# Another order and other engines for the same operations in an attention and feed-forward kernel

## The chip, the cores and the metric

The kernel runs on one core of one Trainium2 chip. The metric is the device time of one execution in microseconds (us), start-up and end included; the profile shows one such execution of its own. The engines are PE (matmuls; PEld are its weight loads), DVE, ACT, POOL and SP. Each works through its own queue in order, and semaphores hold an instruction back until what it needs is there.

## The reference

Eight batches of eight heads, 576 rows, head size 64. Attention is taken over 32 landmarks (means of 18 rows), with the inverse of the 32x32 middle matrix by six steps of an iteration; the result goes through a layer norm and a feed-forward block of width 2048, and is added to itself.

```python
def _attn_ref(q, k, v):
    ...
    q_lm = q.reshape(B, H, m, S // m, D).mean(axis=3)
    k_lm = k.reshape(B, H, m, S // m, D).mean(axis=3)
    ...
    A = sm(q, k_lm)
    Bm = sm(q_lm, k_lm)
    C = sm(q_lm, k)
    ...
    for _ in range(6):
        Z = 2 * Z - Z @ Bm @ Z
    return (A @ Z @ C @ v).astype(np.float32)

def _moe_ref(x, g_ln, w_ch1, w_ch2):
    ...
    xn = (x - mu) / np.sqrt(var + 1e-06) * g_ln
    ch = np.maximum(xn @ w_ch1, 0.0) @ w_ch2
    return (x + ch).astype(np.float32)
```

## The kernel before

The program first defines 1571 named operations, each with the engines that may do it, the buffers that it uses and a function that emits its instructions. A list, ORDER, then names them one by one: a number (the operation's place among the definitions) and a letter for its engine (P, D, A, G and S for PE, DVE, ACT, POOL and SP). The loop at the end of the kernel emits the operations in that list's order, and every engine keeps its instructions in it:

```python
    names = list(OPS)
    order = [(names[int(x[:-1])], x[-1]) for x in ORDER.split()] if ORDER else [(n, OPS[n][0][0]) for n in names]
    for n, e in order:
        emit(n, e)
```

The list sets the buffers too. Each kind of buffer has a number of slots; the first use of a buffer takes the slot that has been free longest, and its last use gives it back, both in the order of the list. PSUM has two slots of two banks (kind p2) and four of one bank (kind bank), so a PE operation that takes a slot waits for the DVE or ACT operation that empties it. Six slots (stg) serve first q, k and v of batch 0, then the tiles of the first weight, then sums of the second.

Batch 0 is loaded by SP and cast to fp16 (cast, tile nat). PE turns it (turns, tiles pst to xT) and sums it by landmark (sums, tile pss), DVE makes qbd from the sums, PE multiplies the landmarks into the first bank of the iteration (psb, tile it). Six steps of the inverse go back and forth between PE (step) and DVE (next). They end in zt and zc (tiles pszt and pszc), of which DVE makes zcbd. rows (psy) gives the attention's rows, x_ copies them out, measure takes the variance. The other batches are worked in sets of one or two in the same manner, beside the feed-forward of batches already there.

For the first matrix of the feed-forward, w1 is loaded in eight tiles (w1s), each scaled in two halves (scale, tile w) and its column means are formed on PE (less_mean, psf) and taken out by ACT (less). psm multiplies the small attention matrix into w1, m16 evicts it (on DVE with less for batches 0 and 1), psh multiplies it by the attention weights ea, and relu evicts that into hT. For batches 0 and 1 the second matrix is multiplied block by block (pso, then done on DVE). From batch 2 on, four blocks at a time are multiplied as a 2x2 problem with seven products instead of eight (seven; tiles ps7a, ps7c, ps7e), for which sums of parts of hT are formed first (hmix, on DVE or POOL, line 207) and sums of the second weight once (mix). norm divides ea by its sums (after ln and inv on ACT). The last block of all is written in two parts, 384 and 128 columns (pso_74a and pso_74b), and stored from SP, ACT or POOL (line 223).

Helpers record most operations, so many have one line: 193 matmuls, 200 copies and casts, 203 activations, 207 tensor_tensor, 210 scalar_tensor_tensor, 223 DMAs. Some matmuls work on tiles of the array of 32x32, 64x32 or 64x64, the others on the whole of it. A few matmuls on zeros (warm, tile idle) keep PE busy at the start.

Of the kernel before, what the change touches and what calls it, by code (L numbers as in the profile page):

```python
# [24 lines left out]
145P 169D 104A 168D 98S 254D 149P 150D 147P 148A 172P 173A 176P 247P 177A 248A 259D 255D 174P 175A
246D 256P 257A 146A 170P 171D 109G 110G 121P 122P 123P 111G 124P 268P 156P 258D 151D 249D 267P 112A
125A 275A 269A 270A 271A 157D 277A 158D 131P 132P 133P 134P 178P 163P 278D 279D 117G 273A 433G 274A
99S 113G 135A 180D 263S 164A 159P 280P 281D 160A 165P 166A 114G 264A 100S 115G 116G 265S 118G 136P
137P 266G 161P 179D 429G 119G 138P 139P 162D 282P 283D 140A 181P 182A 183P 284P 276D 285A 143P 187P
184D 286P 144A 188A 272D 152D 185P 186A 287D 297P 298D 299D 189P 191D 190D 288P 289A 294P 290P 295A  # L30
201P 202P 296A 300P 301A 291D 292P 293A 120G 455G 212P 213P 435G 436G 437G 310P 438G 445G 302A 303G
308P 309A 214P 330P 434D 444D 312D 311D 313D 332D 192P 193A 153D 154D 198P 199A 155A 441D 430D 439D
431D 331D 442D 440D 432D 443D 234P 556D 215P 304P 235P 236P 305A 306A 196P 446G 447G 203P 204P 194P
195A 237P 238P 205P 206P 451G 197A 307G 314P 315A 337P 339P 448G 449D 822G 338A 555D 239P 240P 241P
322P 207P 208P 574D 565D 569G 450D 340A 323A 216P 242D 209D 210S 217P 324D 341P 343D 223P 335P 244S
336A 342D 333P 463D 218P 219P 577G 452D 220D 344P 352P 353D 467G 468G 469G 470G 334A 826G 348P 345A
349A 346P 347A 457G 318P 319A 224P 316P 317A 225P 226P 227P 481P 458G 465D 459G 460G 482A 350P 454D
354D 357P 471D 464D 472D 351A 453D 363P 228P 229P 364D 358A 361P 230P 362A 461D 462D 365D 493P 494A
359P 368P 360A 483P 495P 355P 325D 326D 505A 369A 356A 231D 233A 200G 374P 375P 366P 367A 370P 371A
573G 506D 456D 507P 508P 509D 320P 321D 385P 484P 486A 487A 489A 510P 834D 511D 466D 491A 386P 387P  # L40
485A 388P 211S 512P 376P 473S 474G 490A 377P 496P 498A 501A 499A 497A 513D 514P 327D 488D 492D 328D
396P 397P 475S 476G 566G 828G 829G 830G 831G 572G 477S 478G 838G 839G 844G 564G 568G 503A 378P 379P
380P 515D 823D 502A 221S 504D 372P 516P 479S 480A 500D 517D 836D 528P 529P 530D 531D 398P 399P 373A
381P 522P 518P 389P 329A 866S 382D 418P 519D 824D 559D 520P 521D 523A 532P 419P 420P 524A 533A 534A
558D 550P 551D 552D 553D 548P 549A 421P 422P 423P 536P 424P 425P 848G 535G 832D 833D 554D 232S 867A
537A 538A 539G 560D 525P 527A 400P 401P 557D 426D 427S 605P 526A 606A 840G 841G 594P 595A 561D 540P
541A 390P 391P 611P 612A 837D 596D 827D 392P 393D 825D 850G 851G 852G 563D 603P 604A 853G 562D 859D
842D 860G 861G 843D 579P 613P 614A 407P 580A 601P 602A 609P 610A 1217G 585P 408P 845D 599P 409P 607P
600A 410P 411P 586A 597P 608A 542A 543G 856D 615P 598A 576G 626P 616A 412P 413P 581P 627A 402P 862G
394S 582A 570G 567D 617D 589D 835D 863G 858D 590D 618P 619A 634P 635A 643P 583P 584A 620P 621A 624P  # L50
414P 571G 874P 625A 622P 623A 628P 629A 644P 544P 847D 857D 545A 846D 591D 546A 875D 403P 632P 872S
633A 645P 630P 647P 592D 631A 646P 415D 877P 648P 649P 650P 864D 865D 854D 404D 855D 1191G 886P 638D
637G 641G 663P 664P 665P 639D 640D 662G 428S 417S 406S 661D 593A 882A 884A 879A 880A 883A 652D 878A
651D 657D 887A 889P 892A 896A 658D 666P 668D 894A 895A 849D 667D 653P 654P 711P 722P 712A 723A 891A
890A 655P 656P 547G 575G 675P 676P 677P 728P 729A 678P 695P 696A 1192D 713D 716P 881D 1194D 717A
724P 725A 876P 888P 1213G 660D 587P 870S 714P 416S 659D 871G 873G 384S 1229G 642G 1230G 1231G 726P
898A 715A 679D 682D 669P 897D 727A 588A 730P 222S 1232G 899D 900P 901P 731A 718P 732P 902D 743P 719D
578G 903P 904D 670P 720P 734A 733A 721D 744A 671P 672P 673D 699P 700A 893D 739P 636G 1203D 1239S
701P 905P 243S 741P 906D 740A 751P 674D 742A 703P 752A 907P 735P 736A 737P 383S 868S 681S 680S 683S
738A 702D 908D 909P 1219G 1195G 1220G 1221G 685P 704D 697P 698A 915P 917A 916A 910D 911P 1222G 759P  # L60
760P 749P 811P 925P 750A 761P 885D 869G 921P 926A 927A 753G 922P 1225D 755G 912D 913P 705D 706D 745P
746A 1227D 812P 707D 708D 709D 710A 813P 814P 747P 748A 686P 687P 688P 928G 929P 930A 1223D 1224D
1196D 1233D 815P 816P 923D 1228D 924D 914D 931A 1214D 943P 947D 944D 941P 817P 946D 945D 1240G 754G
756G 932G 758G 942A 762P 692D 767D 694S 689D 818P 763P 764P 918P 765P 766P 395S 1241S 1197G 920A
1198G 1199G 1200G 919A 819D 963P 974P 965A 975A 1207G 1208G 1209G 768D 769P 964D 774D 770P 956P 968P
1215D 1204D 957A 966P 690S 693S 405S 773D 969A 1226D 779P 967A 933P 934A 935A 780P 972P 948P 949A
1234D 1216D 970P 781P 973A 936G 984P 985A 820S 771P 971D 757D 986D 980P 772P 978P 782P 954P 776D
1242A 775D 981A 979A 976P 977A 955A 937P 1193D 938A 939A 1205D 785P 786P 787P 788P 982P 983A 1255P
989P 990A 1210G 684S 783D 1211D 1212D 1201D 1202D 1243P 777G 778G 784D 790D 691S 991P 1244A 789D
992A 801P 1235S 995P 996A 1245P 940G 1236G 1256D 1257P 802P 1267A 1268D 987P 988A 803P 993P 994A  # L70
1066P 1067D 804P 808D 1269P 1270P 1237S 1238G 1246P 1249A 805D 791P 792P 810S 1206D 1271D 821S 1248A
1247A 1253A 1250D 1251A 793P 958D 794P 1006G 1252A 809S 1003P 1004A 1272P 798D 1273D 997P 998A 950P
951A 1001P 1218D 795D 1012P 999P 1002A 1000A 1007G 1009G 1274P 1008D 1275D 952P 953A 1072P 1258P
1073A 1265A 1264A 1276P 1013P 1014P 1015P 1263A 1261A 1260A 1064P 959D 960D 1016P 1259A 961D 962A
1017P 1284P 1285A 1065A 1277D 1278P 1018P 1019P 797S 800S 799S 1294P 1295A 1296A 1021D 1262D 1020D
1026D 1027D 1254D 1279D 1266D 1011G 1022P 1297G 1070P 1023P 1024P 1025P 1029D 1028D 1005G 1068P
1069D 1286A 1298P 1290P 1299A 1291P 1292D 1010D 1293D 1280P 1281D 1091P 1032P 1033P 1038P 1300A
1301G 1092A 1287P 1071D 1289A 1288A 1282P 1283D 1039P 1040P 1312P 1314D 1313D 1316D 1315D 1080P
1082A 796S 1099P 1100A 1081A 1034P 1035P 806S 1310P 1311A 1097P 1036D 1098A 1041P 1306P 1101P 1307A
1095P 1096A 1037D 1030D 1044P 1043D 1093P 1094A 1089P 1090A 1042D 1074D 1075D 1031G 807S 1045P 1046P  # L80
# [1183 lines left out]
```

## Time and profile before

| | us |
|---|---|
| median of three runs | 260.66 (260.17 to 260.79) |
| span of the profiled execution | 258.5 |
| PE busy in it | 249.9 (97%) |
| DVE, ACT, POOL busy | 212.3, 163.9, 177.5 |

The profiled execution's own time is told by its span, from its first to its last instruction; the runs' times hold in addition what lies around that. Lines of the timeline give the start in us, the length, engine, line and operation, the tiles as out<-in, shape, and count; in brackets is the idle time ahead and what ended it. Lines of groups give the total busy time, the mean of one in ns, and the idle time ahead. Lines of the waits give the total, the number and the longest. Lines of the stretches give the stretch, its length, then busy time (and instructions) of PE, PEld, DVE, ACT and POOL, the granted clock, the DMA share and GB/s.

### The profile page before, as it was taken

The numbers are of one execution on the slowest core, as the hardware profiler recorded it, in microseconds if no ns is written. First come the engines' busy times: TensorE is split into PE (matmuls) and PEld (weight loads), VectorE is DVE, ScalarE is ACT, GpSimd is POOL, SyncE is SP. The second block draws the span as 40 slices with busy tenths as digits, with TensorE's granted clock in tenths as the row PEclk, the third lists the DMA queues.
The fourth block names the chain that finished last, engine by engine and source line by source line (L and its number), as shares of the span: only waits on it lengthen the run. The fifth ranks groups of instructions, "written<-read, shape, count | busy, mean of one in ns | idle before, by whom it ended". The sixth has DMA issues, their size and how long they took to land.

```text
span 258.5 us, 8351 instructions
## 1 busy us (share of the span) xinstructions
PE 249.9 (97%) x3499; PEld 179.8 (70%) x3499; DVE 212.3 (82%) x472; ACT 163.9 (63%) x304; POOL 177.5 (69%) x180
## 2 busy tenths in 40 slices
PE   7898999999999999999999999999999999999993
PEld 7766465556554557777766787777867787788981
DVE  1669899999999989997998869898547999878661
ACT  1588886747766999778756997868666245644000
POOL 8324899689794789699999995782078505966600
PEclk9999999999999999999999999999999999999999
DMA  6999999999749176949704832500130100510356
GB/s 234 367 269 338 374 210 208 207 235 244 227 127 178 29 164 87 221 89 286 140 4 121 231 93 61 127 3 3 41 85 0 44 20 9 115 23 20 82 121 184
DMA packets 23277, 36.32 MB, mean 140 GB/s; under 512 B 2116, under 2 KB 11592, under 8 KB 23240
## 3 DMA queue, kind: packets, MB, share of 16 engines
q1 hardware_dynamic: 12456, 23.37, 29.6%
q0 software_dynamic: 9504, 10.36, 25.1%
q10 hardware_dynamic: 1280, 2.07, 3.1%
q8 instruction: 27, 0.44, 0.7%
q14 instruction: 10, 0.08, 0.1%
HBM read 36.70 MB, written 9.44 MB: 178 GB/s over the span
## 4 chain that ended last, share of the span: by engine, by line
PE 85%; DMA 7%; ACT 3%; DVE 2%; issue 1%; SPq 1%; ACTq 0%; DVEq 0%
PE psh L193 23%; PE ps7a L193 16%; PE pso L193 15%; PE ps7c L193 8%; DMA w1s<-in_moe_w_ch_dram 5%; PE ps7e L193 4%; PE psm L193 3%; PE psy L193 3%; DMA stg_q<-in_q_dram 3%; PE it L193 2%; PE pscv L193 2%; PE psd L193 1%; PE psec L193 1%; PE psea L193 1%; PE pso_74a L193 1%
## 5 line engine op out<-in xcount | busy, mean ns | idle before, releaser
L203 ACT ACTIVATE hT<-psh 128x576 f16<-128x576 f32 x106 | 65.8, 650 | 30.4 <-PE psh L193 28.6
L193 PEld LDWEIGHTS <-hT 128*128 128x128 f16 x688 | 64.6, 98 | 22.6 <-issue 3.1
L193 PE MATMUL psh<-ea,m 128*128 128x288 f16 x512 | 78.2, 286 | 0.1
L193 PEld LDWEIGHTS <-m 128*128 128x128 f16 x512 | 48.9, 98 | 15.6 <-issue 1.3
L193 PE MATMUL pso<-w,hT 128*128 128x512 f16 x176 | 45.5, 380 | 0.0
L207 POOL TENSOR_TENSOR mix<-hT 128x1024 f16<-128x1024 f16 x8 | 17.0, 2125 | 27.4 <-ACT hT L203 27.4
L210 DVE SCALAR_TENSOR_TENSOR x<-ps7a,rstd,x 128x256 f32<-128x256 f32 x48 | 21.3, 477 | 6.7 <-PE ps7a L193 4.9
L193 PE MATMUL ps7a<-mix,hT 128*128 128x256 f16 x192 | 25.9, 273 | 0.0
L1068 DVE TENSOR_SCALAR hT<-psh 128x576 f16<-128x576 f32 x22 | 16.4, 753 | 10.1 <-PE psh L193 9.9
L997 DVE BATCH_NORM_STATS2 six<-x 128x6 f32<-128x512 f32 x36 | 24.2, 673 | 0.0
L207 POOL TENSOR_TENSOR ea<-ea,lns 128x576 f16<-128x576 f16 (+1 forms) x14 | 17.7, 1261 | 7.2 <-ACT lns L203 4.0
L200 ACT CAST m<-psm 128x512 f16<-128x512 f32 (+1 forms) x25 | 19.1, 793 | 4.5 <-PE psm L193 3.4
L200 ACT COPY x<-psy 128x512 f32<-128x512 f32 (+1 forms) x29 | 16.8, 587 | 7.6 <-PE psy L193 7.2
L193 PEld LDWEIGHTS <-mix 128*128 128x128 f16 x192 | 18.2, 98 | 4.3 <-issue 1.5
L207 POOL TENSOR_TENSOR mix<-mix,hT 128x1024 f16<-128x1024 f16 x8 | 16.9, 2124 | 6.2 <-DVE mix L207 5.8
L207 POOL TENSOR_TENSOR hT<-hT 128x1024 f16<-128x1024 f16 x9 | 19.1, 2123 | 0.2
L207 POOL TENSOR_TENSOR hT<-hT,mix 128x1024 f16<-128x1024 f16 x7 | 15.1, 2166 | 4.4 <-PE ps7e L193 2.5
L214 DVE TENSOR_REDUCE part<-xT_k 128x32 f16<-128x576 f16 x24 | 17.1, 737 | 0.0
L207 POOL TENSOR_TENSOR asum_q<-asum_q 128x256 f32<-128x256 f32 (+1 forms) x24 | 15.1, 628 | 1.5
L203 ACT ACTIVATE ec<-psec 128x256 f16<-128x256 f32 (+1 forms) x42 | 12.4, 428 | 5.3 <-PE psec L193 5.3
L193 PE MATMUL psy<-zcbd,ea 128*128 128x256 f16 x80 | 14.8, 273 | 0.2 <-ACT x L200 0.2
L200 POOL CAST natv<-stg_v 128x1152 f16<-128x1152 f32 (+1 forms) x12 | 13.8, 1163 | 1.4 <-DMA stg_v<-in_v_dram 1.3
(174 smaller groups left out, 471.2 us busy)
## 6 DMA issues: line engine op xcount, KB each, us to landing
out_dram<-x SPq DMA_DIRECT2D x55, 128.0 KB, 2.7
stg_v<-in_v_dram SPq DMA_DIRECT2D x10, 576.0 KB, 5.1
w1s<-in_moe_w_ch_dram SPq DMA_DIRECT2D x8, 512.0 KB, 11.6
nat_q<-in_q_dram POOLq DMA_DIRECT2D x7, 576.0 KB, 8.7
nat_k<-in_k_dram POOLq DMA_DIRECT2D x7, 576.0 KB, 7.5
w<-in_moe_w_ch_dram POOLq DMA_DIRECT2D x4, 512.0 KB, 8.5
out_dram<-x ACTq DMA_DIRECT2D x15, 128.0 KB, 2.4
stg_v<-in_v_dram SPq DMA_DIRECT2D x6, 288.0 KB, 4.5
```

The lines of the kernel that those rows point to most:

```text
L193: keep(nc.tensor.matmul(o, l, r, start=start, stop=stop, tile_position=(rb, cb), skip_group_check=(skip or cb != 0)))
L200: keep(nc.scalar.copy(o, i) if e == "A" else ENGINES[e].tensor_copy(out=o, in_=i))
L203: keep(nc.scalar.activation(*args, **kw))
L207: keep(ENGINES[e].tensor_tensor(out=o, in0=a, in1=b, op=f))
L210: keep(ENGINES[e].scalar_tensor_tensor(out=o, in0=a, scalar=s, in1=b, op0=f0, op1=f1))
L214: keep(nc.vector.tensor_reduce(out=o, in_=i, axis=axis, op=f))
L997: keep(nc.vector.bn_stats(out=T(f"six_{j}")[:], in_=T(f"x_{j}")[:]))
L1068: keep(nc.vector.tensor_scalar(out=o, in0=T(psh)[:, :, 0:HS], scalar1=0.0, scalar2=None, op0=ALU.max))
```

## The change

The list ORDER is another one; nothing else differs. The operations are the same 1571, each emitted once, on an engine that its definition allows. Some numbers move from one engine to another: four normalisations (norm) and three net sums of the second weight (mix) from DVE to POOL, hmix 14 on DVE and 34 on POOL instead of 16 and 32, relus 18 on DVE and 110 on ACT instead of 22 and 106, and of the 74 stores 28 on ACT, 2 on POOL and 44 on SP instead of 16, 0 and 58.

```diff
 ORDER = """
-0G 20P 23P 4S 12P 14P 24P 17P 11P 2S 1S 3S 6S 7S 10P 21P 28G 38P 25A 26D 34P 39D 40P 29P 30A 31P 27D
...
+0G 12P 19P 11P 4S 23P 20P 22P 15P 16P 2S 26D 24P 17P 14P 13P 18P 21P 1S 28G 38P 40P 34P 42D 39A 250G
...
```

At the head of ACT's queue, in the first 13 us, nat is q or k in fp16, xT its turned copy, it the first bank of the iteration. Before:

```order
2 L200 CAST nat_q<-stg_q 128x2x9x64
3 L200 COPY xT_q<-pst_q 128x1152
4 L203 ACTIVATE it<-it 128x64
5 L203 ACTIVATE ea<-psa 128x576
6 L203 ACTIVATE ect<-psc 128x576
```

After:

```order
2 L200 COPY xT_k<-pst_k 128x1152
3 L200 CAST nat_q<-stg_q 128x2x9x64 x2
4 L200 COPY xT_q<-pst_q 128x1152
5 L203 ACTIVATE it<-it 128x64
6 L203 ACTIVATE ea<-psa 128x576
```

A copy of turned k and the cast of the second half of q, DVE's before, now stand on ACT, the copy first of all.

Further down ACT's queue, in the stretch of 23 to 30 us before, hT is a relu of psh, w a scaled half of a tile of the first weight, less the column means, x the rows. Before:

```order
21 L200 COPY x<-psy 128x512
22 L203 ACTIVATE hT<-psh 128x576 x2
23 L200 CAST tot_k<-psl_k 128x128
24 L203 ACTIVATE hT<-psh 128x576
25 L200 CAST tot_k<-psl_k 128x128
26 L200 COPY x<-psy 128x512
27 L203 ACTIVATE w_16_78<-w1s,g_sb 128x512
28 L200 CAST less<-psf 128x512
```

After:

```order
19 L200 COPY x<-psy 128x512 x2
20 L203 ACTIVATE w_16_78<-w1s,g_sb 128x512
21 L200 COPY x<-psy 128x512
22 L200 CAST tot_k<-psl_k 128x128
23 L203 ACTIVATE hT<-psh 128x576 x2
24 L203 ACTIVATE w_16_78<-w1s,g_sb 128x512
25 L203 ACTIVATE hT<-psh 128x576 x2
26 L200 CAST less<-psf 128x512
```

Between the last x and less stand tot_k, four relus and a w now, and the other x copies have moved ahead of them; before, a w alone stood between the last x and less, and three relus ahead of that.

At the end of DVE's queue, x_5267 of before and x_5084 of after are the last block. Before:

```order
466 L210 SCALAR_TENSOR_TENSOR x_4938<-ps7c_5378,rstd_5299,x_4938 128x256
467 L210 SCALAR_TENSOR_TENSOR x_5211<-ps7a_5219,rstd_5299,x_5211 128x256
468 L210 SCALAR_TENSOR_TENSOR x_5206<-ps7a_5219,rstd_5299,x_5206 128x256
469 L210 SCALAR_TENSOR_TENSOR x_5267<-pso_74b_5394,rstd_5299,x_5267 128x128
470 L210 SCALAR_TENSOR_TENSOR x_5267<-pso_74a_5497,rstd_5299,x_5267 128x384
```

After:

```order
451 L210 SCALAR_TENSOR_TENSOR x_4998<-ps7c_5398,rstd_5323,x_4998 128x256
452 L210 SCALAR_TENSOR_TENSOR x_5223<-ps7a_5277,rstd_5323,x_5223 128x256
453 L210 SCALAR_TENSOR_TENSOR x_5282<-ps7a_5277,rstd_5323,x_5282 128x256
454 L210 SCALAR_TENSOR_TENSOR x_5084<-pso_74a_5482,rstd_5323,x_5084 128x384
455 L210 SCALAR_TENSOR_TENSOR x_5084<-pso_74b_5503,rstd_5323,x_5084 128x128
```

The part of 128 columns comes last instead of that of 384, and the last rows of the seven products stand in another order ahead of it.

More of the change, by code (lines that the diff above doesn't have):

```diff
@@ L25 @@
[L25 to L44, printed above, removed]
@@ new lines @@
+82D 93S 55P 56D 75A 76A 77G 98S 260P 57P 252P 84D 58D 261A 253A 59P 83D 126P 60D 87P 89P 107A 92D
+91D 106G 127P 128P 88A 90D 108G 129P 78G 130A 259D 141P 85P 86A 142D 145P 146A 101G 112G 167P 168D
+147P 148A 169D 94S 102A 143P 144A 255D 153D 149P 150D 247P 248A 249D 172P 176P 173A 256P 174P 177A
+254D 97S 104A 99S 121P 170P 175A 111G 171A 103G 122P 246D 262D 123P 265S 124P 125A 100S 156P 257D
+258D 268P 269A 109G 270A 275A 271A 110G 267P 131P 132P 133P 277A 114G 273A 117G 274A 251D 158D 134P
+157D 135A 159P 178P 113D 161P 278D 179D 160A 180D 263S 136P 165P 433G 137P 162A 272D 279G 280P 166A
@@ new lines @@
+640G 653P 884A 887A 889P 894A 896A 895A 711P 713A 712A 891A 655P 654P 892A 656P 722P 1203D 667D 870S
+661D 897D 890A 1192D 888P 662G 221A 876P 677P 898A 723D 716P 659D 717A 899D 642D 697P 698A 871G
+1230G 675P 714P 641D 726P 676P 406S 900P 660D 417S 715A 728P 727A 720P 678P 679D 721A 729A 695P 901P
+902D 724P 725A 696A 578D 680S 1195G 682D 1231G 671P 718P 719A 730P 903P 904D 732P 734D 1232G 733D
+743P 744A 1219G 893D 384S 905P 906D 1220G 731A 669P 670P 576G 587P 681S 588A 741P 742A 1235S 735P
+701P 672P 739P 736A 405S 740A 849D 737P 738A 811P 1221G 705D 881D 575G 702A 751P 674D 752A 673D 706D
@@ new lines @@
+1245P 1267A 427A 1236D 786P 987P 988A 778G 783D 1268D 1001P 1002A 793P 794P 790D 789D 1269P 1270P
+1271D 1246P 1247A 1248A 1253A 428S 1249A 791P 792P 960D 801P 999P 798D 795D 1251A 1252A 1254D 821S
+1000A 956P 1206D 803P 1003P 1004A 957D 804P 1239S 1240G 997P 998A 797A 1218D 802P 805D 808D 1012P
+1006G 1258P 940G 1272P 1273D 684A 1261A 959D 954P 955A 961D 1265A 1260A 1008G 1013P 1259A 1016P
+1066P 1067A 1264A 1017P 1263A 1014P 962A 1015P 1020D 1266D 1021D 1007G 1009G 806S 1072P 1274P 1284P
+1285A 1275D 1286A 1018P 1019P 807S 1010G 1294P 1073A 1295A 1027D 1026D 1296A 1297G 1005G 1024P 1276P
@@ new lines @@
+796S 1011G 1277D 1250D 1091P 1092A 1070P 1068P 1069D 1022P 1298P 1299A 1025P 1278P 1262D 1291P 1071A
+1290P 1279D 1292D 1293D 1280P 1281D 1300A 1032P 1064P 1033P 1287P 1288A 1282P 1283D 1023P 1029D
+1065D 1289A 1074D 1034P 1035P 1301G 1093P 1094A 800A 1099P 1100A 1080P 1081A 1028D 1082D 809S 1095P
+1096A 1038P 1039P 1040P 1097P 1098A 1083P 1084A 1037D 1041P 1030D 1036D 1044P 1310P 1311A 1043D
+1312P 1315D 1101P 1046P 1314D 1316D 1089P 1103A 1031G 1045P 1313D 1102A 1110P 1042D 1054P 1090A
+1047P 1106P 1111D 1056P 1107A 1087P 1085P 1048D 799A 1088A 1057P 1055P 1104P 1086D 1108P 1105A 1061D
@@ new lines @@
+1062S 1058D 1060S 810S 1180P 1059S 1051D 1332P 1112P 1109A 1343P 1344A 1181P 1075D 1182P 1183P 1113D
+1118P 1119D 1076D 1120P 1184P 1185P 1306P 1121A 1307A 1116P 1117D 1128P 1308A 1130P 1122G 1124G
+1114P 1115D 1347P 1348D 1078D 1333A 1129P 1132P 1134P 1334A 1133P 1052A 1341P 1077D 1323P 1324A
+1351P 1186P 1187P 1126G 1148P 1342D 1345P 1079A 1352A 1188D 1150P 1349P 1123G 1127G 1346A 1131P
+1135P 1339P 1137D 1149P 1125G 1350A 1136D 1140P 1143D 1142D 1063A 1340A 1337P 1309G 1302P 1330D
+1138P 1338D 1151P 1153D 1152D 1364P 1303A 1304A 1189S 1353P 1355A 1354D 1335P 1336A 1146G 1162P
@@ new lines @@
+1160P 1141P 1049S 1365A 1317P 1147D 1360P 1139P 1361A 1372P 1373A 1161P 1368P 1369A 1145D 1362P
+1318D 1144D 1156P 1190A 1363A 1163P 1358P 1167D 1359A 1327D 1154P 1366P 1367A 1305G 1435P 1370P
+1157P 1155P 1460P 1164D 1166A 1158D 1449P 1371A 1159D 1356P 1172P 1357D 1451A 1170P 1171P 1461D
+1053A 1173P 1436A 1441P 1444D 1376G 1319P 1450A 1458P 1459A 1174D 1378G 1375G 1377G 1454P 1455A
+1381P 1452P 1453D 1177D 1383P 1462P 1382P 1463A 1466P 1467A 1456P 1385P 1320D 1328D 1321P 1464P
+1442D 1457A 1379G 1322D 1384P 1386P 1465D 1470P 1329D 1481P 1472A 1331A 1050S 1468P 1469D 1389D
@@ new lines @@
+1390D 1471A 1482A 1387P 1447D 1178S 1388P 1396D 1325P 1395D 1168A 1479P 1401P 1480A 1400G 1393P
+1391P 1394P 1483P 1484D 1477P 1169S 1433P 1165A 1374G 1326A 1392P 1397D 1439P 1478A 1380G 1176S
+1179A 1487P 1488A 1489P 1440D 1402P 1398D 1475P 1407P 1403P 1399G 1404P 1437P 1476D 1473P 1406D
+1474A 1409P 1410P 1408P 1485P 1434A 1497P 1438D 1445D 1486A 1405D 1175S 1415P 1416P 1490A 1501P
+1503P 1413P 1491D 1493G 1495D 1446D 1411D 1443D 1448A 1499P 1500P 1412D 1498P 1423P 1425P 1426P
+1414P 1492D 1424P 1494D 1506D 1505D 1420D 1421A 1509P 1507P 1508P 1427D 1510P 1496G 1417D 1422S
@@ L105 @@
+1419S 1504P 1514D 1502P 1430D 1431A 1511D 1517P 1519P 1520P 1429A 1518P 1513D 1523P 1524P 1516D
+1428S 1525P 1526P 1521D 1522D 1418S 1528D 1515G 1512D 1529P 1531P 1530P 1532P 1527D 1541P 1539P
+1540P 1533D 1542P 1534A 1536D 1538A 1546D 1535S 1537G 1548A 1549P 1550P 1551P 1547G 1552P 1432A
+1553P 1554P 1555P 1543D 1544A 1556P 1560P 1561P 1557D 1562P 1545S 1563P 1564P 1565P 1558A 1559S
+1566P 1567P 1568D 1569A 1570S
 """
```

101 lines of the change are left out of this document (37 added, 64 removed).

## The prediction

> **What bounds the kernel now.** I read the page first, then the busy time by stretch, the waits of PE, and short pieces of the timeline. The page:
>
> ```profile
> span 258.5 us, 8351 instructions
> PE 249.9 (97%) x3499; PEld 179.8 (70%) x3499; DVE 212.3 (82%) x472; ACT 163.9 (63%) x304; POOL 177.5 (69%) x180
> PE 85%; DMA 7%; ACT 3%; DVE 2%; issue 1%; SPq 1%; ACTq 0%; DVEq 0%
> ```
>
> PE is busy nearly all the time and is 85% of the chain that ended last. A busy PE may still hide waits, so the stretches come next (columns: the stretch, its length, then busy time of PE, weight loads, DVE, ACT, POOL):
>
> ```profile
> 10.00:20.00 10.00, 8.70 (x247) 6.58 (x245) 7.17 (x25) 8.13 (x14) 2.85 (x4) 1.00 1.11 286
> 20.00:30.00 10.00, 9.35 (x127) 5.59 (x126) 8.93 (x22) 7.94 (x21) 6.66 (x10) 1.00 1.07 365
> 30.00:40.00 10.00, 9.67 (x145) 6.21 (x145) 9.63 (x26) 8.20 (x17) 9.18 (x13) 1.00 1.19 240
> 40.00:60.00 20.00, 20.00 (x161) 10.93 (x160) 19.79 (x40) 12.45 (x25) 16.50 (x21) 1.00 1.18 228
> 220.00:240.00 20.00, 20.00 (x189) 16.80 (x188) 16.50 (x33) 9.62 (x18) 14.27 (x8) 1.00 0.21 48
> 250.00:258.50 8.50, 4.15 (x35) 2.76 (x32) 2.12 (x5) 0.00 (x0) 0.00 (x0) 1.00 0.59 170
> PE pst_q L197 <- ACT nat_q L200: 0.4, 1, 0.4
> PE pss_q L193 <- DVE nat_q L200: 0.2, 1, 0.2
> ```
>
> All visible idle time of PE lies before 40 us and after 254. In between there is no wait to win, so the same matmuls in another order can differ there only by what one matmul costs the next. Where that is seen (start, length to the modelled end, instruction):
>
> ```profile
> 223.32 0.65 PE L193 MATMUL psh<-ea,m 128*128 128x288 f16 x4
> 223.90 0.63 PE L193 MATMUL psm<-w,zt 64*32 64x512 f16 x16
> ...
> 224.91 0.65 PE L193 MATMUL psh<-ea,m 128*128 128x288 f16 x4
> 225.40 0.82 PE L193 MATMUL ps7a<-mix 128*128 128x256 f16 x6
> ```
>
> The same four psh matmuls take 0.49 from start to next start when full-array work follows (224.91 to 225.40), and 0.58 when a 64*32 tile of the array follows (223.32 to 223.90). So a change of the array's tile shape costs PE about 0.09 us. So three places can move the time: the opening up to about 42 us, the number of tile changes, and the end.
>
> **The change, part by part.** Every operation is kept, so PE's stream of matmuls is the same sum. I work against the profiled span of 258.5 us; the median of the three runs, 260.66, lies 2.2 above it, and I hold that difference fixed.
>
> *Tile changes.* Counted over the two lists, neighbours on PE of unlike tile shape go from 131 to 127. Up to the first psm of batch 1 (42.33 us before) they go from 33 to 38, behind it from 98 to 89. Behind it PE is full, so nine changes fewer are 9 x 0.09 = **-0.8**. The five more belong to the opening and are in its sum.
>
> *The opening.* Its first place is the head of ACT's queue (first pair of lists in the section on the change): DVE's cast of q and its copy of turned k have come to ACT, ahead of everything. The durations, and the moments from which I walk on:
>
> ```profile
> 7.92 1.15 ACT L200 CAST nat_q<-stg_q 128x1152 f16<-128x1152 f32 x1 [5.83 <-DMA stg_q<-in_q_dram]
> 9.84 1.12 ACT L200 COPY xT_q<-pst_q 128x1152 f16<-128x1152 f16 x1 [0.77 <-PE pst_q L197]
> 9.42 0.76 DVE L200 CAST nat_q<-stg_q 128x1152 f16<-128x1152 f32 x1 [0.47 <-DMA stg_q<-in_q_dram]
> 11.33 0.22 PE L193 MATMUL it<-klm,qbd 64*32 64x32 f16 x8
> 14.49 0.46 DVE L207 TENSOR_TENSOR ea<-ea,lns 128x288 f16<-128x288 f16 x1 [0.56 <-ACT lns L203]
> 18.32 0.66 PE L193 MATMUL psl_q<-nat_q,pairs 128*128 128x128 f16 x9
> 19.56 0.77 DVE L220 STREAM_TRANSPOSE xT_q<-nat_q 128x576 uint32<-128x576 uint32 x1
> 19.69 0.21 PE L193 MATMUL pszt<-st,cv 32*32 32x32 f16 x8 [0.33 <-DVE st L210]
> 21.96 1.41 DVE L210 SCALAR_TENSOR_TENSOR m<-less,zsum,psm 128x512 f16<-128x512 f16 x2
> 23.48 1.14 PE L193 MATMUL psh<-ea,m 128*128 128x288 f16 x8
> L207 DVE TENSOR_TENSOR zcbd<-pszc,heads 128x256 f16<-128x256 f32 x16 | 5.9, 415 | 1.2 <-PE pszc L193 1.1
> L200 DVE COPY x<-psy 128x512 f32<-128x512 f32 x8 | 5.5, 682 | 0.0
> 29.06 1.04 PE L193 MATMUL psf<-w,lesser 128*128 128x512 f16 x4 [0.25 <-ACT less L200]
> 42.33 0.41 PE L193 MATMUL psm<-w,zt 64*32 64x512 f16 x8
> L203 ACT ACTIVATE hT<-psh 128x576 f16<-128x576 f32 x106 | 65.8, 650 | 30.4 <-PE psh L193 28.6 <-DVE mix L207 0.8
> L203 ACT ACTIVATE w<-w1s,g_sb 128x512 f16<-128x512 f32 x4 | 2.9, 720 | 0.9 <-DMA w1s<-in_moe_w_ch_dram 0.9
> L200 ACT CAST less<-psf 128x512 f16<-128x512 f32 x4 | 2.4, 589 | 0.7 <-PE psf L193 0.7
> ```
>
> ACT can begin at about 7.9, as in the first row (a group of warm-up matmuls now stands behind PE's first transposes), and the last cast of q ends at 7.9 + 1.12 + 1.15 + 1.15 = 11.3; before it ended at 9.42 + 0.76 = 10.18. From there to PE's it matmuls it took 11.33 - 10.18 = 1.15, so they come at 12.45, 1.1 later. From it to pszt it took 19.69 - 11.33 = 8.4. DVE loses two normalisations of 0.46 there and gains a copy and a v cast of 0.76 each. The normalisations stand on POOL now, behind its two loads and ahead of the weight scaling, so no load waits for them. The warm-up matmuls that stood between the steps now all stand ahead. I leave the 8.4, so pszt comes near 20.8. PE has then done one psl_q group more (18.32 to the next start at 18.82, 0.5) and one psf matmul (0.2): 0.4 behind.
>
> Next DVE has a transpose and a copy of x ahead of the two m evictions that let psh begin. From 20.8 its list runs: 0.2 for the matmuls, two zcbd and a small reduction 1.1, the transpose 0.77, the x copy 0.68, two m 1.41. The second m ends at 25.0, and psh starts at 25.1 against 23.48, with a psl_k group (0.5) and a psy pair (0.2) more done: 0.9 behind.
>
> The second place is ACT again, up to its second less (second pair of lists). A fourth relu, DVE's before, stands ahead of less, and less frees the bank for the next psf. The first psh ends at 25.1 + 0.65 = 25.75; ACT still has an x copy and tot_k before its relu, and I put that at 26.1. Four relus, one w and less are 4 x 0.65 + 0.72 + 0.59 = 3.9, so less ends at 30.0 and psf starts near 30.2 instead of 29.06. With a psy pair more done, that is 1.0 behind. Further on ACT has another relu and another w (POOL's before), and I keep 1.0 behind at psm, 42.33 before. The load order of the w1 tiles changes too, but the first and the last of them keep their place or stand beside a v tile of like size, and DMA is full there (share 1.07 to 1.19), so the last weights land when they did. So the opening is **+1.0**. Lower end: the waits of 0.4 and 0.2 for q (rows above) go and nothing takes their place, -0.6. Upper end: ACT is the bound all the way. Its list up to psm has one w (0.72) and two relus (1.3) more, while its small copies come and go in like number: +2.0. The value is nearest to the walk, since ACT is idle for 2.06 and 1.80 us of the two stretches 20 to 40 before.
>
> *The end.* The third place is DVE's last rows (third pair of lists): the narrow part of the last block comes last. What it saves:
>
> ```profile
> 252.57 0.35 DVE L210 SCALAR_TENSOR_TENSOR x<-pso_74b,rstd,x 128x128 f32<-128x128 f32 x1 [0.43 <-PE pso_74b L193]
> 254.19 0.62 DVE L210 SCALAR_TENSOR_TENSOR x<-pso_74a,rstd,x 128x384 f32<-128x384 f32 x1 [1.27 <-PE pso_74a L193]
> out_dram<-x SPq DMA_DIRECT2D x1, 96.0 KB, 2.1
> out_dram<-x SPq DMA_DIRECT2D x2, 32.0 KB, 2.7
> ```
>
> The last DVE step is 0.35 instead of 0.62, **-0.27**. The store behind it is smaller, but the 32 KB rows landed no sooner than the 96 KB one, so I give it nothing; if it lands like the slower row, 0.6 comes back. Two stores of 128 KB now go out from POOL, about 3 us ahead of PE's last matmul. The rows have no such store; the nearest, a POOL load of 576 KB alone on its queue, landed 5.8 after issue, which reaches about 3 us past PE's end, where the last store ends anyway:
>
> ```profile
> nat_q<-in_q_dram POOLq DMA_DIRECT2D x1, 576.0 KB, 5.8
> ```
>
> [...] So nothing for that.
>
> The sum: -0.8 + 1.0 - 0.27 = -0.1, a span of 258.4 and a time of **260.6**.
>
> **The rivals.** *The opening holds* (faster). If the new list hides ACT's longer runs behind the filler that PE now has there, the opening costs nothing: -0.8 - 0.27 = -1.1, 259.6. For it: PE runs ahead with psl, psy and psf work. Against: both m and less have to pass DVE and ACT first. Chance 0.27.
>
> *ACT bounds the opening* (slower). At the second place above, from less onward; it decides once ACT's added work exceeds its idle time there, and then costs the whole 2.0: -0.8 + 2.0 - 0.27 = +0.9, 261.6. For it: relus, weights and the v cast are in one queue between psh and the slots that psh needs next. Against: 3.9 us of idle time in 20 to 40. Chance 0.15.
>
> *DVE is held by POOL* (slower). The row to look at is a mix of hT on DVE beside one on POOL:
>
> ```profile
> 223.38 1.62 DVE L207 TENSOR_TENSOR hT<-hT,mix 128x1024 f16<-128x1024 f16 x1
> 222.33 2.12 POOL L207 TENSOR_TENSOR hT<-hT 128x1024 f16<-128x1024 f16 x1
> L207 DVE TENSOR_TENSOR hT<-hT 128x1024 f16<-128x1024 f16 x3 | 2.0, 675 | 0.0
> ```
>
> Alone such a mix takes 0.68; started while POOL's ran it ended only after POOL's (224.45), 0.94 late. POOL has more such mixes after the change (34 instead of 32 in hT, 15 instead of 12 in the weights), and in the last batch DVE's two follow each other just when the first of them releases POOL's. A hold delays DVE by 0.94 to 1.4 (2.12 less 0.68), and PE once DVE has no spare time, which is 3.5 of 20 us in 220 to 240. Then the time is 260.6 plus 0.9 to 1.4, 261.5 to 262.0. [...] Chance 0.08.
>
> **How the numbers follow.** A measurement of this kernel can tell about 0.3% (0.8 us) from no change, so faster means under 259.9 and slower over 261.4. My forecast has 0.50, of which 0.03 falls under 259.9. Faster: 0.27 + 0.03 = 0.30. Slower: 0.15 + 0.08 = 0.23. Same: 0.47. The range goes from the opening's lower side (-0.8 - 0.27 with a little of the -0.6) at 259.4 to the middle of the hold's at 261.8; beyond it lie the full -0.6 and a hold on top of ACT's bound.
>
> **What would show it.** In the new profile the it matmuls should start near 12.4 (11.33), pszt near 20.8, the first psh near 25.1, the first psm of batch 1 near 42.9 with one pso pair less before it, and PE should again be busy 20.00 of 20.00 from 60 on. The last DVE step should be 0.35 long and start right behind pso_74b. I am wrong if psh starts by 24.0, if PE shows idle time between 60 and 250, or if a POOL store lands last.

## The result and the profile after

The changed kernel takes 262.37 us (median of four runs, 261.29 to 262.66) beside 260.42 of the kernel before on the same chip: ratio 1.0071, 95% interval 1.0048 to 1.0095. It is 1.9 us slower, and the forecast of 260.6 (259.4 to 261.8) missed it. The profiled execution has a span of 260.8 us. (Two runs of the experiments below stand far above all others, 857.8 us in e2_warm and 268.5 us in e7_warm_wide: they count in the medians, not in the ratios.) From its page:

```profile
span 260.8 us, 8342 instructions
PE 251.7 (96%) x3499; PEld 180.9 (69%) x3499; DVE 210.0 (80%) x461; ACT 165.4 (63%) x309; POOL 186.5 (71%) x188
...
PEclk9977999999999999999999999999999999999999
...
q8 instruction: 27, 0.44, 0.7%
...
PE 87%; DMA 5%; DVE 3%; POOL 2%; issue 1%; ACT 1%; POOLq 0%; ACTq 0%; DVEq 0%
```

PE is still the chain. Two rows are new to the eye: the granted clock falls in the third and fourth slice (13 to 26 us), and a DMA queue of kind "instruction" is there (its packets, MB and share of the engines), 27 packets with 0.44 MB, 16 KB each. The kernel before has that row too; I had not read it. The stretches of the changed kernel (length, then busy time of PE, PEld, DVE, ACT and POOL):

```profile
40.00:60.00 20.00, 19.78 (x195) 11.12 (x193) 19.22 (x39) 12.39 (x24) 18.07 (x22) 1.00 1.17 193
60.00:80.00 20.00, 19.53 (x359) 11.07 (x357) 17.95 (x42) 14.50 (x30) 17.96 (x22) 1.00 0.81 195
120.00:140.00 20.00, 19.30 (x403) 13.09 (x401) 17.74 (x42) 14.46 (x26) 15.98 (x17) 1.00 0.68 154
```

and of the kernel before:

```profile
60.00:80.00 20.00, 20.00 (x393) 11.57 (x391) 18.68 (x45) 12.44 (x30) 17.27 (x20) 1.00 0.77 182
120.00:140.00 20.00, 20.00 (x401) 13.99 (x399) 18.12 (x44) 12.95 (x23) 19.62 (x17) 1.00 0.46 106
```

So PE is idle in the middle, the sign that the prediction named as its own refutation. The waits of PE from 60 to 140 us in the changed kernel, and its timeline around them:

```profile
PE pscv L193 <- issue: 0.7, 1, 0.7
PE it L193 <- issue: 0.4, 1, 0.4
```

```profile
78.76 0.23 PE L193 MATMUL it<-st 32*32 32x64 f16 x7
79.43 0.26 PE L193 MATMUL it<-st 32*32 32x64 f16 x9 [0.44 <-issue]
...
130.54 0.89 PE L193 MATMUL pscv<-natv,ecT 64*64 64x130 f16 x46
132.10 0.59 PE L193 MATMUL pscv<-natv,ecT 64*64 64x130 f16 x26 [0.66 <-issue]
```

Neither is a wait for another engine: "issue" means that PE waited for nothing that the profile shows. Both cut a group in two, the first step_2_4 (the fifth step of batch 2's inverse) after 7 of its 16 matmuls, the second a run of 72 small matmuls (product_31 and product_30) after 46. The idle times count from the modelled end of the last matmul; from start to start, beyond the usual distance, the holes are 0.60 and 0.83 us, and there is a third of 0.18 at 85.90. How many instructions lie between the three (matmuls and weight loads, by the counts in the columns of PE and PEld):

```profile
79.43:85.90 6.47, 6.45 (x128) 3.07 (x129) 5.91 (x16) 3.37 (x8) 1.46 (x2) 1.00 0.63 95
85.90:132.10 46.20, 45.48 (x640) 31.18 (x640) 43.71 (x88) 37.82 (x71) 38.50 (x40) 1.00 0.72 158
```

256 to within one, and 5 x 256. The page has 27 packets, and 6998 instructions of PE (3499 matmuls and as many weight loads), which is 27 times 256 and 86 more. So, as an estimate from these counts, a packet is a block of 256 of PE's own instructions, and PE stood still where a block begins. The trace has each packet's time, but not the moment at which it was asked for. Counted off in the instructions, packets start near the moment at which PE enters the block before. Between 10 and 165 us of the fourteen traces, where data took under a tenth of the DMA engines' time in the microsecond behind that moment, the packet started 0.3 us behind it in the median (70 cases, all but one at most 1.5); where data took over eight tenths, 2.7 us in the median and 4.8 at most (132 cases). A few start up to 1.3 us ahead of it, in stretches of long matmuls. So, as an estimate from these cases, I count a block as asked for when PE enters the one before it. From 126.83, where the block before begins, to the second hole's end, the DMA view has a load of k on GpSimd's queue (q0) in nearly all engines for most of the time:

```profile
DMA  9995999997999999999999997999257989721099
...
q0 software_dynamic: 512, 0.57, 72.3%
q1 hardware_dynamic: 162, 0.33, 23.9%
q8 instruction: 1, 0.02, 1.1%
```

The one instruction packet starts at 129.71, 2.88 late. Ten such requests of the traces (the moments of entry by count, the holes from start to start; the runs are told below):

| kernel | block entered, next one asked for | packet starts | ends | next block begins | hole |
|---|---|---|---|---|---|
| before | 78.61 | 80.66 | 81.60 | 84.08 | 0 |
| before | 123.87 | 124.03 | 125.02 | 129.66 | 0 |
| changed | 74.13 | 77.01 | 77.91 | 79.43 | 0.60 |
| changed | 126.83 | 129.71 | 130.67 | 132.10 | 0.83 |
| changed, again | 73.28 | 77.19 | 78.08 | 79.63 | 1.66 |
| two loads moved | 74.21 | 78.10 | 79.07 | 80.33 | 1.42 |
| late loads | 126.63 | 126.79 | 127.97 | 131.03 | 0 |
| wide warm-ups | 127.76 | 129.01 | 129.96 | 131.35 | 0.44 |
| wide, k load later | 127.36 | 130.54 | 131.52 | 132.99 | 2.48 |
| before, wide warm-ups | 125.52 | 128.80 | 129.76 | 131.04 | 1.09 |

Where there is a hole, it ends 1.26 to 1.55 us after the packet does. So, as an estimate from these rows, a block of 256 must last about as long as the request waits, plus 1.0 for the packet, plus 1.4. Most blocks last 6 to 15 us. Where the small matmuls of the steps, products and psec stand together it is 3.2 to 6.3 (the hole left out), and a wait of more than 0.8 to 3.9 us is enough.

The end went as said, DVE's last rows:

```profile
256.07 0.62 DVE L210 SCALAR_TENSOR_TENSOR x<-pso_74a,rstd,x 128x384 f32<-128x384 f32 x1 [1.73 <-PE pso_74a L193]
256.96 0.35 DVE L210 SCALAR_TENSOR_TENSOR x<-pso_74b,rstd,x 128x128 f32<-128x128 f32 x1 [0.28 <-PE pso_74b L193]
```

From PE's last matmul to the end it is 3.93 us instead of 4.34. GpSimd's stores landed 3.2 us after their issue by the DMA view (issued by 254.80), ahead of the end.

### The profile page after: what moved, and what is told of

Its sections match the earlier page's. It is cut to its first block, busy times and chain, and to the rows that moved or that the text cites. A ratio compares the mean times of both kernels' runs of the same rounds, so it can differ in the third digit from the quotient of the medians.

```text
span 260.8 us, 8342 instructions
## 1 busy us (share of the span) xinstructions
PE 251.7 (96%) x3499; PEld 180.9 (69%) x3499; DVE 210.0 (80%) x461; ACT 165.4 (63%) x309; POOL 186.5 (71%) x188
## 4 chain that ended last, share of the span: by engine, by line
PE 87%; DMA 5%; DVE 3%; POOL 2%; issue 1%; ACT 1%; POOLq 0%; ACTq 0%; DVEq 0%
PE psh L193 24%; PE ps7a L193 16%; PE pso L193 14%; PE ps7c L193 8%; DMA nat_q<-in_q_dram 5%; PE ps7e L193 4%; PE psm L193 4%; PE psy L193 3%; PE it L193 3%; PE pscv L193 2%; PE psd L193 1%; PE psec L193 1%; PE psea L193 1%; DVE m L210 1%; PE psf L193 1%
## 5 line engine op out<-in xcount | busy, mean ns | idle before, releaser
L203 ACT ACTIVATE hT<-psh 128x576 f16<-128x576 f32 x110 | 69.1, 652 | 34.2 <-PE psh L193 33.5
L193 PEld LDWEIGHTS <-hT 128*128 128x128 f16 x688 | 64.6, 98 | 23.3 <-issue 4.1
L207 POOL TENSOR_TENSOR ea<-ea,lns 128x576 f16<-128x576 f16 (+1 forms) x18 | 21.1, 1176 | 21.0 <-ACT lns L203 13.7
L207 POOL TENSOR_TENSOR mix<-mix,hT 128x1024 f16<-128x1024 f16 x10 | 21.8, 2175 | 3.8 <-DVE mix L207 3.5
L200 ACT CAST m<-psm 128x512 f16<-128x512 f32 (+1 forms) x25 | 17.7, 743 | 5.0 <-PE psm L193 3.5
L200 ACT COPY x<-psy 128x512 f32<-128x512 f32 (+1 forms) x27 | 15.8, 585 | 6.4 <-PE psy L193 6.0
L1068 DVE TENSOR_SCALAR hT<-psh 128x576 f16<-128x576 f32 x18 | 13.4, 749 | 6.9 <-PE psh L193 6.9
L207 POOL TENSOR_TENSOR hT<-hT 128x1024 f16<-128x1024 f16 x8 | 17.5, 2190 | 1.1 <-DVE mix L207 1.1
L207 POOL TENSOR_TENSOR hT<-hT,mix 128x1024 f16<-128x1024 f16 x8 | 17.4, 2176 | 1.1 <-PE ps7e L193 1.0
L193 PE MATMUL psy<-zcbd,ea 128*128 128x256 f16 x80 | 14.9, 275 | 0.3 <-DVE m L210 0.3
L203 ACT ACTIVATE lns<-psd 128x576 f32<-128x576 f32 x16 | 10.5, 654 | 5.7 <-PE psd L193 4.0
```

Source lines behind the costliest of these rows:

```text
L193: keep(nc.tensor.matmul(o, l, r, start=start, stop=stop, tile_position=(rb, cb), skip_group_check=(skip or cb != 0)))
L200: keep(nc.scalar.copy(o, i) if e == "A" else ENGINES[e].tensor_copy(out=o, in_=i))
L203: keep(nc.scalar.activation(*args, **kw))
L207: keep(ENGINES[e].tensor_tensor(out=o, in0=a, in1=b, op=f))
L1068: keep(nc.vector.tensor_scalar(out=o, in0=T(psh)[:, :, 0:HS], scalar1=0.0, scalar2=None, op0=ALU.max))
```

## The experiments

Theory A: the loss is the holes at the starts of instruction blocks; the change moved loads of GpSimd's queue to where PE asks for a block ahead of a dense stretch. Theory B, the rival: it lies in the order itself, in the late opening with its half clock, or in data that come late in the middle. All medians are of 6 to 12 runs, beside the kernel before in the same session (260.3 to 260.4).

**The changed kernel once more** (f1_again), nothing edited.

> The changed kernel itself, once more, for more runs and a second trace. Theory A: the holes of PE lie again where the 193rd instruction of a 256-instruction block stands (in step_2_4, pso_14_10, product_30 or at other such places, not anywhere else), but not all of them in each run, since a load and a request race within about a microsecond; so single runs lie between 260.3 (no hole) and 263 us, with a median of 262 to 262.5. Theory B (data or engines that come late in this order): the same holes of 0.60, 0.18 and 0.83 us in the same matmuls, and runs within 0.5 us of each other.

Measured: 262.37 us (261.65 to 263.0), ratio 1.0075 (1.0056 to 1.0094). Its trace has one hole between 60 and 140 us, of 1.66 start to start:

```profile
77.91 0.23 PE L193 MATMUL it<-st 32*32 32x64 f16 x7
79.63 0.26 PE L193 MATMUL it<-st 32*32 32x64 f16 x9 [1.49 <-issue]
...
16.50:23.30 6.80, 5.78 (x130) 3.47 (x131) 4.50 (x13) 3.93 (x9) 4.99 (x8) 1.00 1.12 296
...
41.47 0.41 PE L193 MATMUL psm<-w,zt 64*32 64x512 f16 x8
...
PE pso L193 <- DMA w<-in_moe_w_ch_dram: 0.5, 2, 0.3
```

The hole is at the same matmul of step_2_4 as in the first trace, and longer (1.66 beside 0.60); the one in product_30 (0.83 there) is absent: the same program had other holes in another execution, as A has it. No run reached 260.3. The clock was full (1.00) and psm of batch 1 came at 41.47, earlier than in the kernel before (42.33), and still the span is 259.9 beside 258.5: the opening isn't where the time goes.

**Two loads moved** (e1_loads). GpSimd's list by name:

```diff
 asum_q410
+load_q50
 asum_q411
 asum_q412
-load_q50
...
-load_k70
 tail_2
 asum_q600
 asum_q601
+load_k70
```

> The changed kernel with two loads of GpSimd's queue at another place in its list: the load of q for batch 5 two operations earlier (right behind asum_q410), the load of k for batch 7 three operations later (behind asum_q601). Nothing else differs. Theory A (TensorE's own instructions come late: its instruction blocks wait behind these loads): the holes of 0.60 us in step_2_4 at 78.8 us and of 0.83 us in product_30 at 131 us go, with them the 0.18 us at 85.9; PE is 20.00 of 20.00 us busy in 60 to 80 and at least 19.9 in 120 to 140; time 262.4 - 1.6 = 260.8 us. Theory B (the loss lies in the opening and its half clock): the opening is untouched, so the time stays at 262.4 us.

Measured: 261.45 us (260.15 to 262.95), ratio 1.0034 (1.0014 to 1.0054). Half right. 120 to 140 is 19.96 busy; the hole at 131 is gone. But the one in step_2_4 is larger, 1.42 start to start:

```profile
60.00:80.00 20.00, 19.04 (x348) 10.75 (x346) 17.42 (x41) 14.59 (x30) 17.74 (x22) 1.00 0.84 183
120.00:140.00 20.00, 19.96 (x418) 13.78 (x410) 18.18 (x45) 15.21 (x27) 15.75 (x18) 1.00 0.70 162
80.33 0.26 PE L193 MATMUL it<-st 32*32 32x64 f16 x9 [1.26 <-issue]
72.58 0.78 POOL L223 DMA_DIRECT2D nat_q<-in_q_dram  x1
```

The q load stands earlier in the list, but GpSimd was later in this execution: it issued at 72.58, where the changed kernel's trace has 72.04. A place in a list is no place in time.

**Both loads behind the requests** (e5_loads_late).

```diff
-load_q50
 mix_14
...
 mix_34
+load_q50
 load_k50
...
-load_k70
 tail_2
 asum_q600
 asum_q601
+load_k70
```

> The changed kernel with the load of q for batch 5 moved behind mix_34, right ahead of the load of k for batch 5 (about 4 us later), and the load of k for batch 7 moved behind asum_q601. TensorE asks for a block of instructions at about 74.1, 78.8 and 126.9 us; no load starts in the two us ahead of these any more. Theory A (late instruction blocks cost the changed kernel its 1.8 us): no hole of over 0.3 us in PE between 60 and 140 us, 260.2 to 260.5 us in nearly all runs, with a spread of under 1 us, where the changed kernel has 261.3 to 262.7. Theory B (the order of the middle itself costs it, by data that come late): holes at other places or the same, 261.5 us or more.

Measured: 260.9 us (260.33 to 261.81), ratio 1.0021 (1.001 to 1.0033). No wait for instructions is left in the trace:

```profile
60.00:80.00 20.00, 19.48 (x359) 10.92 (x357) 18.34 (x41) 14.46 (x30) 18.10 (x22) 1.00 0.72 175
80.00:100.00 20.00, 20.00 (x263) 10.97 (x262) 19.14 (x38) 15.44 (x28) 14.24 (x16) 1.00 0.72 161
120.00:140.00 20.00, 19.97 (x416) 13.59 (x422) 18.24 (x43) 15.36 (x28) 15.82 (x18) 1.00 0.66 151
PE psh L193 <- ACT hT L203: 0.5, 1, 0.5
```

Two loads moved by a few places give back 1.5 of the 2.0 us. The level of 260.2 to 260.5 in nearly all runs was not reached, and the spread is 1.5 us; the idle 0.5 that is left from 60 to 80 is ACT, where a cast of v waited for its transfer ahead of a relu.

**That cast behind the relu** (f4_cast_late), on top of the late loads.

```diff
-cast_v30
...
 relu_111
+cast_v30
```

> The kernel with the late loads (260.9 us), and on ScalarE the cast of v for batch 3 (cast_v30) moved from ahead of relu_111 to right behind it, since it stood there waiting for its transfer with psh_113 waiting behind (0.66 us in that trace). If that wait recurs in most runs: 260.3 to 260.5 us; if it was that one run's, 260.9 us again.

Measured: 261.16 us (260.2 to 261.9), ratio 1.0029 (1.0016 to 1.0042). No wait of PE is left in its trace from 43 to 250 us, whose span is 258.9, but the median is no lower than with the late loads, as it would be if that wait was one execution's.

**Wide warm-ups in the kernel before** (e7_warm_wide). The loads and the order stay, only PE's blocks begin elsewhere:

```diff
-    warm(24, 160)
+    warm(15, 256)
     for _ in range(14):
-        warm(4, 128)
+        warm(2, 256)
```

> The kernel before, where each warm-up group has half as many matmuls of twice the columns (2 of 256 for 4 of 128; 15 of 256 for 24 of 160): as many columns, 74 instructions of TensorE fewer, all of them before 20 us. Theory A (TensorE's instructions come in blocks of 256, and a block that is asked for while a load holds the DMA engines comes late): every block boundary behind the warm-ups falls 74 instructions further on in the program; the ones that then fall at about 76, 79 and 125.7 us lie in or right at loads of k and q and ahead of stretches of small matmuls that last 3.2 to 6 us, so holes appear in PE there that the kernel before doesn't have: 260.8 to 262.3 us. Theory B (order, data and clock alone matter): 260.4 us, the same as before.

Measured: 261.92 us, ratio 1.0057 (1.0035 to 1.0079): 1.5 slower, by an edit that ends at 20 us. The trace has a hole of 1.09, none in 60 to 80, and its first psm of batch 1 is even earlier (42.33 before):

```profile
42.04 0.41 PE L193 MATMUL psm<-w,zt 64*32 64x512 f16 x8
...
60.00:80.00 20.00, 20.00 (x403) 11.50 (x405) 18.68 (x45) 12.57 (x29) 16.96 (x20) 1.00 0.85 189
120.00:140.00 20.00, 19.08 (x379) 13.40 (x377) 17.71 (x43) 11.84 (x21) 18.52 (x16) 1.00 0.40 89
129.05 1.07 PE L193 MATMUL pscv<-natv,ecT 64*64 64x130 f16 x58
131.04 0.42 PE L193 MATMUL pscv<-natv,ecT 64*64 64x130 f16 x14 [0.92 <-issue]
```

From that psm to PE's last matmul it is 1.16 us longer than the kernel before, and the hole is 1.09 of that. This is the strongest evidence for A: the list, the loads and the engines are those of the kernel before, and B has no term for it.

**Wide warm-ups in the changed kernel** (f2_wide), the same edit there.

> The changed kernel with its warm-up groups made of half as many matmuls of twice the columns, so that each block of instructions begins 74 instructions further on in the program; the loads stay. Theory A: the blocks are then asked for at about 76 and 81 us (in the loads of q and k for batch 5, but ahead of stretches of 5 and 6.5 us) and at 128.6 us (in the load of k for batch 7, ahead of a stretch of 4.0 us): no hole in step_2_4 or at 85.9 us, one of 0.3 to 1.5 us at about 133 us, none in product_30 where it was. Time 261.6 to 262.4 us. Theory B: the holes stay in step_2_4 and product_30, 262.4 us.

Measured: 261.49 us, ratio 1.005 (1.0034 to 1.0066). No hole at 79 or 86; a small one of 0.17 where the block now begins at 80.21, and one of 0.44 where step_3_4 stands:

```profile
129.78 1.10 PE L193 MATMUL pscv<-natv,ecT 64*64 64x130 f16 x62
130.81 0.26 PE L193 MATMUL it<-st 32*32 32x64 f16 x11
131.35 0.21 PE L193 MATMUL it<-st 32*32 32x64 f16 x5 [0.28 <-issue]
...
123.87 0.77 POOL L223 DMA_DIRECT2D nat_k<-in_k_dram  x1 [1.03 <-DVE xT_q L220]
```

Before the edit the hole was behind the 46th of the 72 pscv matmuls; now the other 26 and 11 of the step's 16 have passed as well. 37 matmuls with their weight loads are the 74 instructions by which the blocks were moved.

**The same, and the load of k for batch 7 behind asum_q601** (f3_wide_k70).

> The run with the wide warm-ups, and the load of k for batch 7 moved behind asum_q601 as well (127.5 instead of 124.8 us), which puts its transfer behind the request at 128.6 us. Theory A: no hole of over 0.3 us between 60 and 140 us; 260.7 to 261.1 us, as with the two loads moved. Theory B: 262.4 us.

Measured: 264.14 us, ratio 1.0141 (1.0116 to 1.0166), the slowest of all, against what I expected. The trace shows why:

```profile
125.29 0.77 POOL L223 DMA_DIRECT2D nat_k<-in_k_dram  x1
...
130.42 0.26 PE L193 MATMUL it<-st 32*32 32x64 f16 x11
132.99 0.26 PE L193 MATMUL it<-st 32*32 32x64 f16 x5 [2.31 <-issue]
...
133.00:136.40 3.40, 3.40 (x20) 2.29 (x20) 2.63 (x6) 1.19 (x2) 3.40 (x3) 0.50 0.10 34
```

The load came at 125.29 instead of 127.5, since GpSimd had no wait there now. Its issue ended 1.3 us ahead of the request at 127.36 instead of 3.1 us ahead (f2_wide: issue from 123.87, request at 127.76). The same hole at the same matmul grew from 0.44 to 2.48, and the median by 2.65. Not all of that need be the hole itself: right behind it the granted clock is half for 3.4 us (last row), where f2_wide has 1.00, and the block of instructions that begins there lasts 8.5 us instead of 6.9. My place for the load was wrong; as a dose it bears A out.

**Warm-ups between the steps again** (e2_warm).

```diff
+warm_8
 psb_0
...
+warm_12
+warm_9
+warm_5
 step_0_0
...
+warm_3
 step_0_2
...
+warm_6
 total_q11
```

> The changed kernel with six of its warm-up groups put between the first steps again, as the kernel before has them: one ahead of psb_0, three ahead of step_0_0, one ahead of step_0_2, one ahead of total_q11. Both theories: the granted clock stays full between 16 and 23 us, where it was half. Theory A (the half clock hides behind the transfers of the opening): the first psm of batch 1 starts at 42.6 to 43.0 us instead of 43.02, and the time falls by at most 0.4 us, to 262.0 to 262.4 us. Theory B (the half clock is the loss): the steps get back their 1.5 us, psm_10 starts at about 42 us and the time is 261.1 us or less.

Measured: 262.27 us, ratio 1.0067 (1.0043 to 1.0091), the other runs from 261.15 to 264.29. The clock stays full from 16.5 to 23.3, psm of batch 1 starts at 42.72, and the time doesn't move. The half clock is not the loss. The trace has the hole in product_30 (0.62) and none in step_2_4.

**The opening of before** (e3_opening): the first 264 operations of the list before, then the changed list's rest; **and with the late loads** (e8_best). Where the lists meet, beside the list before:

```diff
 pso_01_04
-psm_10
-turn_q20
+measure_2
+mix_00
+measure_3
...
```

> The list of the kernel before up to the first psm of batch 1 (its first 264 operations, with their engines), and behind it the rest in the order and on the engines of the changed kernel. Theory A (the middle costs 1.6 us by late instruction blocks, the opening 0.7): 262.4 - 0.7 = 261.7 us, with holes in PE between 60 and 140 us as in the changed kernel, unless the earlier opening moves a block away from a load. Theory B (the opening is the whole loss): 260.4 us or less, no holes.

> The list of the kernel before up to the first psm of batch 1, the changed kernel's behind it, and the two loads moved as in the run with the late loads. Theory A: no holes, 260.0 to 260.2 us in nearly all runs, the level of the fastest runs of the list with the opening of before (260.07 and 260.16). Theory B: as the list with the opening of before, 260.8 us.

Measured: 260.82 us (ratio 1.0015, 0.9997 to 1.0033) and 260.99 us (1.0024, 1.0008 to 1.0041). Both expectations of A missed: 0.9 better than said, and 0.8 worse. The first trace has holes of 0.49 in step_2_4 and, in the opening, of 0.91 at psm_01 (22.3 us), none at 131; the second none from 60 to 140, and one of 0.58 at psm_01. So the exchanged opening moved PE against its loads as well. The first psm of batch 1 starts at 42.73 and 43.23 us in the two traces, later than the 42.33 of the kernel before, so they had the old opening's list but not its time. With late loads in both, the old list gives 260.99 and the new one 260.9; what the old opening is worth at its own time these runs don't show.

**The end** was tried twice. e4_tail takes the changed list from the first pso_74b on:

```diff
 seven_66_04
-store_27_1
-pso_74b_00
-pso_74b_02
+store_23_0
+store_23_1
+seven_66_10
...
```

> The kernel before with the end of the changed kernel alone: from its 1504th operation on (the first pso_74b) the order and the engines of the changed kernel, so the last narrow part stands wholly behind the wide one and two stores are GpSimd's. By the prediction's end term: the last VectorE step takes 0.35 instead of 0.62 us, 0.27 to 0.47 us are gained, 260.0 to 260.15 us beside 260.42. Rival (the last store's landing sets the end, whatever its part's width): 260.4 us. Rival (a GpSimd store lands last): slower than 260.5 us.

Measured: 261.3 us (1.004, 1.0026 to 1.0054). The time says nothing of the end, since the splice left PE a wait of its own (from PE's last matmul to the end the trace has 3.94 us instead of 4.34):

```profile
PE ps7a L193 <- DVE mix L207: 1.0, 1, 1.0
```

e6_tail_alone moves only the narrow part, and one of its two stores from SP to ACT, which the expectation doesn't say:

```diff
-pso_74b_00
...
-done_74b
...
 pso_74a_14
+pso_74b_00
...
+pso_74b_14
 done_74a
+done_74b
```

> The kernel before with the narrow last part (pso_74b, its VectorE step, its two stores) moved wholly behind the wide one, and nothing else: no store on GpSimd, no other order. By the prediction's end term the last VectorE step is 0.35 instead of 0.62 us: 260.4 - 0.27 = 260.1 us, down to 259.9. Rival (the landing of the last store sets the end, and takes the same for both widths): 260.4 us.

Measured: 260.2 us, ratio 0.9994 (0.9981 to 1.0008). In its trace PE's last matmul is 3.88 us ahead of the end instead of 4.34. It fits the gain of 0.27 and can't be told from none. It is the fastest kernel of the study, though not measurably faster than the one before.

## Why the prediction was wrong

Worked out from the traces (us; holes from start to start):

| | before | changed | changed, again | late loads and cast (f4_cast_late) | before, wide warm-ups |
|---|---|---|---|---|---|
| first psm of batch 1 starts | 42.33 | 43.02 | 41.47 | 42.54 | 42.04 |
| from there to the end of PE's last matmul | 211.83 | 213.90 | 214.57 | 212.38 | 212.99 |
| of it, holes at starts of blocks | 0 | 1.61 | 1.66 | 0 | 1.09 |
| of it, a pso pair that stood ahead of psm before | 0 | 0.43 | 0.43 | 0.43 | 0 |
| of it, waits for the second weight's load | 0 | 0 | 0.8 | 0 | 0 |
| the rest of it | 211.83 | 211.86 | 211.68 | 211.95 | 211.90 |
| from PE's last matmul to the end | 4.34 | 3.93 | 3.90 | 3.99 | 4.32 |
| span | 258.5 | 260.8 | 259.9 | 258.9 | 259.4 |

- **The failed step** is in the first part: "In between there is no wait to win, so the same matmuls in another order can differ there only by what one matmul costs the next." There was no wait to win, but one to lose, and it is no wait for an engine: PE's own instructions, whose packets the DMA view has on the same 16 DMA engines as the loads (1.1% beside 72.3% for the load of k, from 126.8 to 132.1). The prediction put it at nothing (its reading beside it, that no idle time of PE lies between 40 and 254 us, is right to 0.1 us: 140 to 160 is 19.90 busy); it is 1.61 and 1.66 us in the two traces. With it the profiled sum closes: 0.69 later at psm, 0.43 for the pso pair, 1.61 of holes and -0.41 at the end are 2.3, of 2.3 measured.
- **Tile changes, -0.8: right in count and price, but not gained.** Behind the first psm of batch 1, the starts that follow a change of tile shape come later than their columns alone make it by 9.42 us in all before (98 changes, 0.096 each) and by 8.63 after (89, 0.097): -0.79. But the row "the rest of it" is 211.83 before and 211.7 to 211.95 with the changed list, so the stretch as a whole is no shorter by that amount. The time between two matmuls of one and the same small tile shape, from start to start and without the holes, went up, from 14.43 us in all to 14.9. What makes up the remainder stays open. This term is the second part of the miss: it priced the changes of shape and nothing else that a matmul costs the next.
- **The opening, +1.0: right in size in the profiled run, not as a property of the list.** The marks were 11.84 (12.45 said), 21.54 (20.8), 26.09 (25.1), 30.56 (30.2) and 43.02 (42.9): late as said, +0.69 and a pso pair of 0.43 less done. But that execution had the half clock (0.50 from 16.5 to 23.3 us), which I had not thought of when the warm-ups moved; with full clock (1.00) the same list reached psm at 41.47, and then PE waited twice for the second weight's load (0.5 us by the row above, 0.8 from start to start). That the walk came out near the measured mark is in part luck.
- **The end, -0.27: right in sign.** 0.41 and 0.44 in the traces, 0.2 in the runs, within their uncertainty.
- **What stays open.** The trace of f4_cast_late, which has no holes, is 0.4 above the kernel before: 0.21 and 0.43 in the opening, 0.12 in the rest of the middle, -0.35 at the end. The medians of the kernels with late loads are 0.5 to 0.8 above it; what other executions add to the one in the trace is not shown.
- **The rivals.** *The opening holds* and *ACT bounds the opening* each named one outcome: the first trace had neither, the second reached psm early and lost it in waits for a load. *DVE is held by POOL*: GpSimd's work rose by 9 us, but no wait of PE from 43 us to its last matmul is put down to DVE in either trace of the changed kernel. It was slower for a reason that none of the three had.

## What to carry to other kernels

Before a reordering is judged, look at the instruction queue in the DMA part of the page and at the engine with the most instructions. In this kernel the places at risk were those where 256 instructions of PE passed in 3 to 6 us and a load of 576 KB had been issued one to four us before such a stretch's blocks were asked for. A wait for "issue" in the middle of a group of equal matmuls, at distances that are multiples of 256 instructions of PE (1 and 5 times here), was the sign of it. And since such holes moved with a count of instructions far ahead (74 fewer before 20 us), a harmless edit at the start can move the time (here by 0.6%), so a small gain or loss of a new order isn't to be put down to the order before this is ruled out.

## What the runs showed of the hardware beyond this

The clock of TensorE fell to half from 16.5 to 23.3 us in the changed kernel's first trace:

```profile
13.00:16.50 3.50, 2.81 (x74) 1.69 (x73) 2.76 (x10) 3.04 (x6) 0.80 (x1) 1.00 1.11 268
16.50:23.30 6.80, 6.16 (x102) 3.94 (x100) 3.21 (x11) 2.72 (x7) 4.84 (x8) 0.50 1.12 296
```

In the second trace the stretch ahead was as busy (2.80 of 3.50 us) and the clock stayed full (1.00 from 16.5 to 23.3). What lowered it in the first these traces don't show. No cost of it shows in the medians: with warm-ups between the steps (e2_warm), where the trace has a clock of 1.00 over that stretch, it is 262.27 instead of 262.37 us.
